# Moving the second scores and AV three matmuls later, giving group 0 a fourth output tile, and sharing the first half's products with GpSimd

## The chip, the cores and the metric

The kernel runs on one core of a Trainium2 chip. A core has five engines with instruction streams of their own: TensorE (PE in the profile, with its weight loads as PEld), VectorE (DVE), ScalarE (ACT), GpSimd (POOL) and SyncE (SP), which here only issues DMA transfers. The metric is the device time of one execution in microseconds (us). It was 322.27 us, the median of three runs (321.61 to 323.1).

## The reference: hourglass attention, then a feed-forward layer

The inputs are `q`, `k` and `v` of 8 batches, 8 heads, 576 positions and 64 elements a head. Two attentions are computed for each head and added:

```
q_d, k_d, v_d = means over 4 neighbouring positions     # 144 positions
out_up    = repeat(softmax(q_d @ k_d.T / 8) @ v_d, 4)   # back to 576
scores    = where(|i - j| < 4, q @ k.T / 8, -1e9)
out_local = softmax(scores) @ v                         # a band of 7
x = (out_up + out_local), heads side by side            # 4608 tokens x 512
out = (h * sigmoid(1.702 * h)) @ w_out, with h = x @ w_in   # 512 -> 2048 -> 512
```

The second part is the MoE of the names in the kernel, a feed-forward layer with one expert. Its matmuls are most of the work.

## The kernel before

**MoE.** The 4608 tokens are handled in nine groups of 512, 0 to 8. `mm1` multiplies `w_in` (the weights, 128 columns at a time: 16 blocks `ffc`) with `xT`, four matmuls of 128x128 by 512 a block, one for each of the four tensors `xT[0..3]` (`dmc`), which hold 128 columns of `x` each, transposed. ScalarE applies SiLU from PSUM into `gT` (L858). `mm2` multiplies `gT` with `w_out`: four output tiles of 128 tokens, 16 matmuls each (L919). `store` copies a tile from PSUM to a buffer `osb` on ScalarE (L904) and SP's queue writes it out (L909). There are three such buffers. One group is 128 of these matmuls.

**Attention.** Batch 0 is done at the start. Batch b is computed while group b - 1 runs its MoE, so groups 0 to 6 carry an attention and groups 7 and 8 do not. From group 1 on (batches 2 to 7) the steps are hung between MoE matmuls at the counts in `POS`: a count below 16 stands ahead of that block of `mm1`, a count of 16 + n ahead of matmul n of `mm2`. The five steps are: the scores of the first four heads (12), their Exp and mask (16), the scores, Exp and mask of the other four heads (33), the attention times V (AV) of the first half, `avx` for `xT[0]` and `xT[1]` (41), and of the second half, for `xT[2]` and `xT[3]` (53). Group 0 has counts of its own (`POS_0`) and another AV.

**PSUM.** Three pairs of banks, PA[0] to PA[2], serve the scores and AV. Each block of scores fills all three: the pooled scores in PA[0], the local ones in PA[1] and PA[2]. ScalarE empties them with one Exp for `ed` (L450) and two for `es` (L444), and VectorE multiplies `es` with the mask (L458). An AV block fills all three again, with numerators and denominators: PA[0] and PA[2] are the main parts (`mains(par)`), PA[1] is the rest. Two further banks, PM, and the PA banks take the MoE's sums.

**The tail of an AV block** (L758 to L791). ScalarE takes Ln of the denominators into `l` (L762, L764), and one Exp of -`l` over all 1440 columns makes their inverses (L768). VectorE copies the numerators into `n` (L763, L767); these copies are ordered behind the Ln that reads the same banks. `l` has two buffers, `n` one. Then nine products of `n` and `l` on VectorE (L773) make `od`, the pooled part, and the eight pieces of the two `xT`; two adds bring `od` into each `xT` (L789), on GpSimd for the first half and on VectorE for the second. After the second half ScalarE loads the table for SiLU again (L770). The next group's `mm1` reads `xT[0]` and `xT[1]` in its first eight matmuls, `xT[2]` in the next four, then `xT[3]`.

**Order.** Each engine works through its instructions in the order of the program; waits on other engines are added where data or buffers demand it. VectorE goes on with the transposes of the next batch's `k` and `q` (L284) behind the second half's adds; GpSimd sums them over four positions (L315, L319), issues the next loads, and prepares `vb` and `vd` (L325, L332, L335), which the next AV reads.

Of the kernel before, what the change touches and what calls it, by code (L numbers as in the profile page):

```python
# [8 lines left out]
FP32 = mybir.dt.float32  # L9
BF16 = mybir.dt.bfloat16  # L10
AF = mybir.ActivationFunctionType
ALU = mybir.AluOpType
# [7 lines left out]
def kernel(  # L20
# [9 lines left out]
    nc = tc.nc  # L30
    B, H, S, D = q.shape
# [655 lines left out]
    def avx(b, hps):  # L687
        vb, vd = vbs[b % 2], vds[b % 2]

        def mains(par):  # L690
            return PA[2 * par]

        def down(kc, den):
            for u, hp in enumerate(hps):
                rows = slice(64 * u, 64 * u + 48)
                for j in range(2):
                    nc.tensor.matmul(  # L697
                        mains(u)[64 * j : 64 * j + 64, den, DN : DN + SD],
                        lhsT=ones[rows, 1, :] if den else vd[rows, kc, hp // 2 * 2 + j, 0:D],
                        rhs=eds[hp // 2][rows, j, SD * kc : SD * kc + SD],  # L700
                        start=(kc == 0), stop=(kc == 2),
                        tile_position=(64 * u, 64 * j),
                    )

        def local(den, to, what):
            for par in range(2):
                hp = hps[par] if to == "main" else hps[1 - par]
                i, c0, ni, n = what[par]
                rows = slice(64 * par, 64 * par + 64)
                if to == "rest":  # L710
                    t, bk = PA[1], par
                    at = 256 * den + 57 * (i - 1 + par)
                else:
                    t, bk = mains(par), den
                    at = 57 * i + c0 if par == 0 else 57 * i
                    if to == "extra":
                        at = EX
                for j in range(2):
                    nc.tensor.matmul(  # L719
                        t[64 * j : 64 * j + 64, bk, at : at + ni * n],  # L720
                        lhsT=ones[rows, 0, :] if den else vb[rows, i, 2 * hp + j, 0:D],
                        rhs=sub(es[hp][rows, j, :], 60 * i + c0, (60, ni), (1, n)),
                        start=True, stop=True,
                        tile_position=(64 * par, 64 * j),
                    )

        def rest(k):
            local(0, "rest", ((k + 1, 3, 1, 57), (k, 0, 1, 57)))

        def rest_den(k):  # L730
            local(1, "rest", ((k + 1, 3, 2, 57), (k, 0, 2, 57)))

        def main(k):
            local(0, "main", ((k, 3 if k else 0, 1, 57 if k else 60),
                              (k, 0, 1, 57 if k < 4 else 60)))

        def extra(den):
            local(den, "extra", ((0, 0, 1, 60), (4, 0, 1, 60)))

        for kc in range(3):  # L740
            down(kc, 0)
            rest(kc)
            down(kc, 1)
            if kc < 2:
                rest_den(2 * kc)
        rest(3)
        main(0)
        local(1, "main", ((1, 3, 2, 57), (0, 0, 2, 57)))
        main(1)
        local(1, "main", ((3, 3, 2, 57), (2, 0, 2, 57)))  # L750
        main(2)
        local(1, "main", ((0, 0, 1, 60), (4, 0, 1, 60)))
        main(3)
        extra(0)
        main(4)
        extra(1)

        l = work.tile([128, 2, S + SD], FP32, name="l", tag="l", bufs=2)  # L758
        n = work.tile([128, 2, S + SD], FP32, name="n", tag="n", bufs=1)
        od = work.tile([128, 2, SD], FP32, name="od", tag="od", bufs=2)  # L760
        for par in range(2):
            nc.scalar.activation(out=l[:, par, 0:RS], in_=mains(par)[:, 1, 0:RS], func=AF.Ln)  # L762
            nc.vector.tensor_copy(out=n[:, par, 0:RS], in_=mains(par)[:, 0, 0:RS])  # L763
        nc.scalar.activation(  # L764
            out=l[:, :, RS : S + SD], in_=PA[1][:, :, 256 : 256 + S + SD - RS], func=AF.Ln
        )
        nc.vector.tensor_copy(out=n[:, :, RS : S + SD], in_=PA[1][:, :, 0 : S + SD - RS])  # L767
        nc.scalar.activation(out=l, in_=l, func=AF.Exp, scale=-1.0)  # L768
        if hps[0]:
            nc.scalar.preload_act_table_set("silu_and_others")  # L770

        def mult(out, *part):
            nc.vector.tensor_tensor(out=out, in0=sub(n, *part), in1=sub(l, *part), op=ALU.mult)  # L773

        t0, W = b * S, S + SD
        mult(od, DN, (W, 2), (1, SD))
        xa, xb = (xT[hp] for hp in hps)
        mult(sub(xa, t0 + 3, (114, 5), (1, 57)), 3, (57, 5), (1, 57))
        mult(sub(xa, t0 + 60, (114, 4), (1, 57)), W + RS, (57, 4), (1, 57))
        mult(sub(xa, t0 + 516, (1, 60)), W + EX, (1, 60))  # L780
        mult(sub(xa, t0, (1, 3)), 0, (1, 3))
        mult(sub(xb, t0 + 60, (114, 5), (1, 57)), W, (57, 5), (1, 57))
        mult(sub(xb, t0 + 117, (114, 4), (1, 57)), RS, (57, 4), (1, 57))
        mult(sub(xb, t0, (1, 60)), EX, (1, 60))
        mult(sub(xb, t0 + 573, (1, 3)), W + 285, (1, 3))
        for u, hp in enumerate(hps):
            xs = xT[hp][:, t0 : t0 + S].rearrange("p (t f) -> p t f", f=4)
            eng = nc.vector if hps[0] else nc.gpsimd
            eng.tensor_tensor(  # L789
                out=xs, in0=xs, in1=sub(od[:, u, :], 0, (1, SD), (0, 4)), op=ALU.add  # L790
            )  # L791

# [93 lines left out]
    def mm2(g, gT, steps):  # L886
        tok0 = g * TG
        turn["m"] = 1
        n = 0

        if g == 0:
            order = [(t0 + u, 4 * c + f)
                     for t0, c in ((0, 0), (0, 1), (2, 0), (2, 1),
                                   (0, 2), (2, 2), (0, 3), (2, 3))
                     for u in range(2) for f in range(4)]
        else:
            order = [(t, ffc) for t in range(4) for ffc in range(n_ffc)]
        ops = {}

        def store(t, ap, c0, n, eng, q):  # L900
            r0 = tok0 + 128 * t
            osb = moe_sb.tile([128, n], FP32, name="osb", tag=f"osb{n}", bufs=3)
            if eng is nc.scalar:
                eng.activation(out=osb, in_=ap, func=AF.Copy, scale=1.0 / GELU_SCALE)  # L904
            else:
                eng.tensor_single_scalar(  # L906
                    out=osb, in_=ap, scalar=1.0 / GELU_SCALE, op=ALU.mult
                )
            q.dma_start(out=out[r0 : r0 + 128, c0 : c0 + n], in_=osb)  # L909

        for t, ffc in order:
            if g == n_groups - 1 and t == 3:
                continue
            for f in steps.get(n, ()):
                f()
            n += 1
            if ffc == 0:
                ops[t] = PB[0][:, t - 2, :] if g == 0 and t > 1 else pm_tile()
            nc.tensor.matmul(  # L919
                ops[t],  # L920
                lhsT=gT[:, ffc, t * 128 : (t + 1) * 128],
                rhs=w_out_bf[:, ffc, :],
                start=(ffc == 0), stop=(ffc == n_ffc - 1),
            )
            if ffc == n_ffc - 1 and not (g == 0 and t == 2):
                for u in (2, 3) if g == 0 and t == 3 else (t,):
                    store(u, ops[u], 0, d_model, nc.scalar, nc.sync)

        if g == n_groups - 1:
            for h in range(2):  # L930
                cols = slice(256 * h, 256 * h + 256)
                p = pm_tile()
                for ffc in range(n_ffc):
                    nc.tensor.matmul(
                        p[:, 0:256],
                        lhsT=gT[:, ffc, 384:512],
                        rhs=w_out_bf[:, ffc, cols],
                        start=(ffc == 0), stop=(ffc == n_ffc - 1),
                    )
                if h == 0:  # L940
                    store(3, p[:, 0:256], 0, 256, nc.scalar, nc.sync)
                else:
                    store(3, p[:, 0:128], 256, 128, nc.scalar, nc.scalar)
                    store(3, p[:, 128:256], 384, 128, nc.vector, nc.sync)
        for f in steps.get(n, ()):
            f()

    POS = [12, 16, 33, 41, 53]
    POS_0 = [16, 18, 27, 46, 50, 55, 64, 68, 73]
    VDP_0 = 41  # L950

# [164 lines left out]
```

## Time and profile before

| what | us |
|---|---|
| median of three runs | 322.27 |
| the profiled execution | 321.51 |
| its span, first to last instruction | 319.7 |
| TensorE matmuls busy | 300.3 (94%) |
| ScalarE busy | 200.4 (63%) |
| GpSimd busy | 156.7 (49%) |
| VectorE busy | 143.0 (45%) |
| TensorE's granted clock, mean | 0.993 |

The engines work side by side, so their busy times do not add up. Lines of the profile name the source line, the engine, the operation, and output <- input by the program's names; "x8" counts instructions in a line, and a bracket tells how long the engine had been idle and what ended that. In a timeline the first two numbers are the start, in us from the span's start, and the time to the last end of the merged instructions. In the list of waits they are the total, the count and the longest. In the list of instruction groups the numbers behind the bar are the busy time in us, the mean of one in ns, and the idle time ahead.

### The profile page before, as it was taken

The numbers are of one execution on the slowest core, as the hardware profiler recorded it, in microseconds if no ns is written. First come the engines' busy times: TensorE is split into PE (matmuls) and PEld (weight loads), VectorE is DVE, ScalarE is ACT, GpSimd is POOL, SyncE is SP. The second block draws the span as 40 slices with busy tenths as digits, with TensorE's granted clock in tenths as the row PEclk, the third lists the DMA queues.
The fourth block names the chain that finished last, engine by engine and source line by source line (L and its number), as shares of the span: only waits on it lengthen the run. The fifth ranks groups of instructions, "written<-read, shape, count | busy, mean of one in ns | idle before, by whom it ended". The sixth has DMA issues, their size and how long they took to land.

```text
span 319.7 us, 10088 instructions
## 1 busy us (share of the span) xinstructions
PE 300.3 (94%) x4389; PEld 153.9 (48%) x4434; DVE 143.0 (45%) x283; ACT 200.4 (63%) x321; POOL 156.7 (49%) x183
## 2 busy tenths in 40 slices
PE   6779998989999999999999999999999999999995
PEld 2454454434554555454545454545454544444444
DVE  6973524740299048903791379226931580000000
ACT  4474782366795589558856875687577758315611
POOL 8973960099334973398239913992298030000000
PEclk9989999999999999999999999999999999999999
DMA  6999999979705991399349934794330120020011
GB/s 118 122 203 211 173 131 213 202 198 225 150 35 165 195 190 49 126 205 172 98 129 191 196 83 125 167 198 107 107 110 3 53 84 2 9 89 35 0 66 66
DMA packets 64124, 39.98 MB, mean 125 GB/s; under 512 B 44624, under 2 KB 54992, under 8 KB 64080
## 3 DMA queue, kind: packets, MB, share of 16 engines
q0 software_dynamic: 18864, 14.95, 33.1%
q1 hardware_dynamic: 45072, 24.32, 30.6%
q8 instruction: 34, 0.56, 0.7%
q14 instruction: 10, 0.08, 0.1%
q10 hardware_dynamic: 144, 0.07, 0.1%
HBM read 44.83 MB, written 9.44 MB: 170 GB/s over the span
## 4 chain that ended last, share of the span: by engine, by line
PE 75%; DMA 9%; ACT 6%; POOL 5%; issue 4%; DVE 0%; POOLq 0%; ACTq 0%
PE pm L919 28%; PE pm L847 22%; PE pa L847 12%; DMA kb<-in_k_dram 4%; PE pa L409 3%; PE pa L719 2%; DMA qb<-in_q_dram 2%; ACT es L444 2%; ACT L813 2%; PE pa L697 2%; PE pa L919 2%; ACT ed L450 2%; POOL vb L237 2%; DMA vb<-in_v_dram 1%; PE pa L433 1%
## 5 line engine op out<-in xcount | busy, mean ns | idle before, releaser
L919 PE MATMUL pm<-w_out_bf,gT 128*128 128x512 bf16 x503 | 114.6, 379 | 3.3 <-issue 2.9
L847 PE MATMUL pm<-xT,w_in_bf 128*128 128x512 bf16 x361 | 92.2, 380 | 1.7 <-ACT gT L858 1.3
L847 PEld LDWEIGHTS <-w_in_bf 128*128 128x128 bf16 x576 | 55.6, 98 | 67.7 <-issue 1.7
L858 ACT ACTIVATE gT<-pm 128x512 bf16<-128x512 f32 x94 | 56.2, 602 | 42.9 <-PE pm L847 42.9
L919 PEld LDWEIGHTS <-gT 128*128 128x128 bf16 x560 | 52.6, 98 | 60.9 <-issue 0.2
L458 DVE TENSOR_TENSOR es<-es,mask 128x600 bf16<-128x600 bf16 x28 | 19.8, 722 | 89.7 <-ACT es L444 89.0
L847 PE MATMUL pa<-xT,w_in_bf 128*128 128x512 bf16 x199 | 53.2, 379 | 0.4
L904 ACT ACTIVATE osb<-pm 128x512 f32<-128x512 f32 (+2 forms) x35 | 20.4, 582 | 33.1 <-PE pm L919 27.6
L789 POOL TENSOR_TENSOR xT<-xT,od 128x576 bf16<-128x576 bf16 x12 | 16.8, 1396 | 43.9 <-DVE xT L773 43.6
L315 POOL TENSOR_TENSOR pq<-kT 128x576 f32<-128x576 bf16 x14 | 16.2, 1157 | 39.0 <-DVE kT L284 38.9
L858 ACT ACTIVATE gT<-pa 128x512 bf16<-128x512 f32 x50 | 29.0, 607 | 5.6 <-PE pa L847 5.6
L773 DVE TENSOR_TENSOR xT<-n,l 128x285 bf16<-128x285 f32 (+1 forms) x96 | 28.2, 366 | 0.0
L906 DVE TENSOR_SCALAR osb<-pm 128x128 f32<-128x128 f32 x1 | 0.3, 292 | 53.7 <-ACT osb L904 53.7
L332 POOL TENSOR_TENSOR pq<-v 112x512 f32<-112x512 f32 x18 | 23.7, 1318 | 0.0
L444 ACT ACTIVATE es<-pa 128x600 bf16<-128x600 f32 x32 | 19.7, 670 | 2.1 <-PE pa L391 2.1
L284 DVE STREAM_TRANSPOSE kT<-kb 128x576 f32<-128x576 f32 x16 | 19.9, 1247 | 1.6 <-DMA kb<-in_k_dram 1.5
L284 DVE STREAM_TRANSPOSE qT<-qb 128x576 f32<-128x576 f32 x16 | 19.9, 1241 | 0.3 <-DMA qb<-in_q_dram 0.2
L763 DVE COPY n<-pa 128x492 f32<-128x492 f32 x24 | 15.0, 665 | 8.9 <-ACT l L762 8.3
L762 ACT ACTIVATE l<-pa 128x492 f32<-128x492 f32 x24 | 12.6, 578 | 10.0 <-PE pa L719 10.0
L450 ACT ACTIVATE ed<-pa 128x864 bf16<-128x864 f32 x16 | 14.3, 891 | 4.5 <-PE pa L433 4.4
L768 ACT ACTIVATE l<-l 128x1440 f32<-128x1440 f32 x12 | 16.8, 1403 | 0.4
L237 POOL DMA_DIRECT2D vb<-in_v_dram x20 | 13.8, 701 | 5.3 <-DMA w_in_bf<-in_moe_w_in_dram 3.3
(119 smaller groups left out, 353.6 us busy)
## 6 DMA issues: line engine op xcount, KB each, us to landing
out_dram<-osb SPq DMA_DIRECT2D x35, 256.0 KB, 2.4
vf<-in_v_dram SPq DMA_DIRECT2D x60, 128.0 KB, 6.3
v<-in_v_dram SPq DMA_DIRECT2D x72, 96.0 KB, 3.2
kb<-in_k_dram POOLq DMA_DIRECT2D x16, 288.0 KB, 6.5
qb<-in_q_dram POOLq DMA_DIRECT2D x16, 288.0 KB, 8.5
w_out_bf<-in_moe_w_out_dram POOLq DMA_DIRECT2D x4, 512.0 KB, 13.7
vb<-in_v_dram POOLq DMA_DIRECT2D x20, 64.0 KB, 5.4
w_in_bf<-in_moe_w_in_dram POOLq DMA_DIRECT2D x2, 512.0 KB, 8.1
```

Source lines behind the costliest of these rows:

```text
L237: nc.gpsimd.dma_start(out=vbs[b % 2][64 * par : 64 * par + 64, i, :, 0:D], in_=bass.AP(tensor=v.tensor, offset=v[b, 0].offset + (114 * i + ...
L284: nc.vector.transpose(out=t32.rearrange("p (i c) -> p c i", c=18), in_=store[b, qd].bitcast(FP32).rearrange("p (c d) -> p c d", c=18),)
L332: eng.tensor_tensor(out=t1[0:112], in0=x[:, :, 0:2, :], in1=x[:, :, 2:4, :], op=ALU.add)
L444: nc.scalar.activation(out=es[2 * qd + u][:, :, 0:300], in_=sp[u][:, :, 0:300], func=AF.Exp, scale=inv_sqrt_d,)
L450: nc.scalar.activation(out=eds[qd][:, :, 0:432], in_=sd[:, :, 0:432], func=AF.Exp, scale=inv_sqrt_d / 16.0,)
L458: nc.vector.tensor_tensor(out=ev, in0=ev, in1=mask, op=ALU.mult)
L768: nc.scalar.activation(out=l, in_=l, func=AF.Exp, scale=-1.0)
L773: nc.vector.tensor_tensor(out=out, in0=sub(n, *part), in1=sub(l, *part), op=ALU.mult)
L847: nc.tensor.matmul(acc, lhsT=w_in_bf[:, dmc, ffc * 128 : (ffc + 1) * 128], rhs=xT[dmc][:, g * TG : g * TG + TG], start=(dmc == 0), stop=(d ...
L858: nc.scalar.activation(out=gT[:, ffc, :], in_=acc, func=AF.Silu, scale=GELU_SCALE)
L904: eng.activation(out=osb, in_=ap, func=AF.Copy, scale=1.0 / GELU_SCALE)
L919: nc.tensor.matmul(ops[t], lhsT=gT[:, ffc, t * 128 : (t + 1) * 128], rhs=w_out_bf[:, ffc, :], start=(ffc == 0), stop=(ffc == n_ffc - 1),)
```

## The change

Three counts of `POS` grow by three, so the second scores and both AV blocks of groups 1 to 6 come three MoE matmuls later. In group 0 the third output tile is copied into the buffer of `n`, which group 0 does not otherwise use, so that four output tiles have four buffers. In the AV tail, the first half (`second` false) alternates Ln and copies over the bank pairs and gives `od`, the four pieces of `xT[1]` and the two adds to GpSimd; VectorE keeps the four pieces of `xT[0]`. The second half (`second` true) keeps all products and adds on VectorE, and its Exp of -`l` is done in two parts. TensorE's instructions stay the same in number; GpSimd gets 30 more, VectorE 30 fewer, ScalarE six more.

```diff
-        for par in range(2):
+        second = hps[0] > 0
+        W = S + SD
+
+        def ln_main(par):
             nc.scalar.activation(out=l[:, par, 0:RS], in_=mains(par)[:, 1, 0:RS], func=AF.Ln)
+
+        def ln_rest():
+            nc.scalar.activation(
+                out=l[:, :, RS:W], in_=PA[1][:, :, 256 : 256 + W - RS], func=AF.Ln
+            )
+
+        def copy_main(par):
             nc.vector.tensor_copy(out=n[:, par, 0:RS], in_=mains(par)[:, 0, 0:RS])
-        nc.scalar.activation(
-            out=l[:, :, RS : S + SD], in_=PA[1][:, :, 256 : 256 + S + SD - RS], func=AF.Ln
-        )
-        nc.vector.tensor_copy(out=n[:, :, RS : S + SD], in_=PA[1][:, :, 0 : S + SD - RS])
-        nc.scalar.activation(out=l, in_=l, func=AF.Exp, scale=-1.0)
-        if hps[0]:
+
+        def copy_rest():
+            nc.vector.tensor_copy(out=n[:, :, RS:W], in_=PA[1][:, :, 0 : W - RS])
+
+        def inverse(c0, c1):
+            ap = l[:, :, c0:c1]
+            nc.scalar.activation(out=ap, in_=ap, func=AF.Exp, scale=-1.0)
+
+        if second:
+            ln_main(0)
+            ln_main(1)
+            inverse(0, RS)
+            ln_rest()
+            inverse(RS, W)
             nc.scalar.preload_act_table_set("silu_and_others")
-
-        def mult(out, *part):
-            nc.vector.tensor_tensor(out=out, in0=sub(n, *part), in1=sub(l, *part), op=ALU.mult)
-
-        t0, W = b * S, S + SD
-        mult(od, DN, (W, 2), (1, SD))
+            copy_main(0)
+            copy_main(1)
+            copy_rest()
+        else:
+            ln_main(0)
+            copy_main(1)
+            ln_main(1)
+            copy_rest()
+            ln_rest()
+            copy_main(0)
+            inverse(0, W)
+
+        def mult(eng, out, *part):
+            eng.tensor_tensor(out=out, in0=sub(n, *part), in1=sub(l, *part), op=ALU.mult)
+
+        t0 = b * S
         xa, xb = (xT[hp] for hp in hps)
-        mult(sub(xa, t0 + 3, (114, 5), (1, 57)), 3, (57, 5), (1, 57))
-        mult(sub(xa, t0 + 60, (114, 4), (1, 57)), W + RS, (57, 4), (1, 57))
...
+        ea = nc.vector
+        eb = nc.vector if second else nc.gpsimd
+        mult(eb, od, DN, (W, 2), (1, SD))
+        mult(ea, sub(xa, t0 + 3, (114, 5), (1, 57)), 3, (57, 5), (1, 57))
+        mult(ea, sub(xa, t0 + 516, (1, 60)), W + EX, (1, 60))
+        mult(ea, sub(xa, t0, (1, 3)), 0, (1, 3))
+        if second:
+            mult(ea, sub(xa, t0 + 60, (114, 4), (1, 57)), W + RS, (57, 4), (1, 57))
+        mult(eb, sub(xb, t0 + 60, (114, 5), (1, 57)), W, (57, 5), (1, 57))
+        mult(eb, sub(xb, t0, (1, 60)), EX, (1, 60))
+        mult(eb, sub(xb, t0 + 573, (1, 3)), W + 285, (1, 3))
+        if not second:
+            mult(ea, sub(xa, t0 + 60, (114, 4), (1, 57)), W + RS, (57, 4), (1, 57))
+        mult(eb, sub(xb, t0 + 117, (114, 4), (1, 57)), RS, (57, 4), (1, 57))
         for u, hp in enumerate(hps):
             xs = xT[hp][:, t0 : t0 + S].rearrange("p (t f) -> p t f", f=4)
-            eng = nc.vector if hps[0] else nc.gpsimd
-            eng.tensor_tensor(
+            eb.tensor_tensor(
                 out=xs, in0=xs, in1=sub(od[:, u, :], 0, (1, SD), (0, 4)), op=ALU.add
             )
...
         def store(t, ap, c0, n, eng, q):
             r0 = tok0 + 128 * t
-            osb = moe_sb.tile([128, n], FP32, name="osb", tag=f"osb{n}", bufs=3)
+            if g == 0 and t == 2:
+                osb = work.tile([128, 2, S + SD], FP32, name="n", tag="n", bufs=1)
+                osb = osb[:, 0, 0:n]
+            else:
+                osb = moe_sb.tile([128, n], FP32, name="osb", tag=f"osb{n}", bufs=3)
...
-    POS = [12, 16, 33, 41, 53]
+    POS = [12, 16, 36, 44, 56]
```

More of the change, by code (lines that the diff above doesn't have):

```diff
@@ L780, in avx @@
[L780 to L785, printed above, removed]
+        def ln_rest():
+            nc.scalar.activation(
+                out=l[:, :, RS:W], in_=PA[1][:, :, 256 : 256 + W - RS], func=AF.Ln
+            )
```

## The prediction

> **What bounds the kernel now.** I read the page first, then who waited for whom on TensorE, the chain that ended last, and the timelines of one group (group 3, whose MoE starts at 129.6 us) engine by engine.
>
> ```profile
> span 319.7 us, 10088 instructions
> PE 300.3 (94%) x4389; PEld 153.9 (48%) x4434; DVE 143.0 (45%) x283; ACT 200.4 (63%) x321; POOL 156.7 (49%) x183
> ...
> PE pm L847 <- ACT gT L858: 1.3, 1, 1.3
> PE pa L409 <- ACT es L444: 0.9, 6, 0.2
> ```
>
> TensorE is busy for 94% of the span, so the change can win only what TensorE still waits for. The first wait line is one wait of 1.3 us, the second comes once in each of six groups. The chain shows what the first stands behind:
>
> ```profile
> 61.23 3.37 DMA out_dram<-osb
> 64.68 0.60 ACT osb L904
> 65.81 7.71 PE pm L847 x35
> ```
>
> Group 0 has four output tiles and three buffers. The fourth copy waits for a buffer until the first tile has been written out, holds up ScalarE, and with it the first SiLU of group 1. Now the second wait, in the PE and ACT timelines:
>
> ```profile
> 147.19 1.24 PE L919 MATMUL pm<-w_out_bf,gT 128*128 128x512 bf16 x5
> 148.77 0.22 PE L409 MATMUL pa<-qT,kT 32*64 32x60 bf16 x4 [0.15 <-ACT es L444]
> 150.08 1.67 PE L919 MATMUL pm<-w_out_bf,gT 128*128 128x512 bf16 x7 [0.16 <-issue]
> ...
> 147.50 1.23 ACT L444 ACTIVATE es<-pa 128x600 bf16<-128x600 f32 x2
> ```
>
> The second scores reach TensorE at 148.27 but need the banks that the two Exp leave at 148.73. Counted between MoE matmul starts, less the slots of 0.216 us, the first scores cost 1.13 us of TensorE (groups 1 to 6 agree), the second 1.56, 1.62, 1.59, 1.57, 1.59, 1.48. So the wait is worth 0.44 us a group, 2.62 us in all. The two AV blocks cost 1.21 and 1.20 us: no wait is left in them.
>
> The third thing to see is the tail, from the first AV block to the next group's xT:
>
> ```profile
> 156.30 2.85 DVE L773 TENSOR_TENSOR xT<-n,l 128x285 bf16<-128x285 f32 x8
> 159.25 1.25 DVE L763 COPY n<-pa 128x492 f32<-128x492 f32 x2
> 161.32 1.83 DVE L773 TENSOR_TENSOR xT<-n,l 128x285 bf16<-128x285 f32 x8
> 163.07 1.42 DVE L789 TENSOR_TENSOR xT<-xT,od 128x576 bf16<-128x576 bf16 x2
> ...
> 157.34 1.35 POOL L789 TENSOR_TENSOR xT<-xT,od 128x576 bf16<-128x576 bf16 x1 [6.06 <-DVE xT L773]
> 159.23 1.21 POOL L789 TENSOR_TENSOR xT<-xT,od 128x576 bf16<-128x576 bf16 x1 [0.54 <-DVE xT L773]
> ...
> 164.15 0.38 PE L847 MATMUL pm<-xT,w_in_bf 128*128 128x512 bf16 x1
> ```
>
> The same eight products take 1.83 us alone and 2.85 us while GpSimd adds: one 228-element product that begins at 157.54 lasts 1.40 us instead of 0.39, until GpSimd's add is over. VectorE and GpSimd, with two SBUF operands each, run one after the other. The second half's xT2 is ready at 163.82, and the next group's matmul that reads it starts at 164.15. The tail has 0.33 us to spare and no more.
>
> **The change, part by part.** Times are from A, the start of the MoE matmul behind the first AV block (152.79 in group 3).
>
> Output tile. ScalarE is free at 63.95 instead of 65.28. The first SiLU then waits only for its matmuls (their end, 64.33), runs 0.60 us, and TensorE goes on at 65.01 instead of 65.81. The rest of that stop (64.38 to 65.01) stays, since group 1 begins with two banks. Gain 0.80 us; bounds 0 and 1.4 (the whole stop). SP's queue keeps its order. `n` is a single buffer, so group 1's first copy waits for that store, which has 20 us to land: nothing.
>
> Second scores. They come 3 slots (0.65 us) later, at 148.92, behind the Exp's end at 148.73. The wait goes: gain 2.62 us, bounds 0 and 2.62. What is late next: the first AV block, still eight matmuls behind, wants bank PA2, which the second scores' Exps leave. They start 0.82 us after the scores (149.83), take 2.02 us (149.63 to 151.65 before), and end at 151.85; AV starts at 151.87. I take 0.02 us a group, bounds 0 and 0.3.
>
> AV later. Both blocks move with the scores, 12 matmuls apart as before, but only 24 instead of 27 matmuls follow the second. So xT2 is needed at A + 12 x 0.2163 + 1.20 + 24 x 0.2163 + 8 x 0.2163 = A + 10.72, against A + 11.36 before.
>
> Reading the banks. In the first half Ln and copies now take turns on a bank pair. VectorE starts with ScalarE instead of behind it: last copy at A + 2.0 instead of A + 2.5, and the second AV starts at A + 2.69. Ln waits for copies in turn, so the Exp ends at A + 3.37 instead of A + 3.04. Products start 0.09 later, as before: A + 3.45.
>
> Products. VectorE keeps 4 (half of the 8 at 161.32, 0.88 us), GpSimd gets five, 288, 285, 60, 3 and 228 elements. The trace has no such product on GpSimd. The nearest rows:
>
> ```profile
> L319 POOL TENSOR_TENSOR qdT<-pq 128x288 bf16<-128x288 f32 x13 | 8.7, 667 | 1.0
> L332 POOL TENSOR_TENSOR pq<-v 112x512 f32<-112x512 f32 x18 | 23.7, 1318 | 0.0
> L335 POOL TENSOR_TENSOR vd<-pq 112x256 bf16<-112x256 f32 x18 | 13.5, 753 | 1.4
> ```
>
> From L319 (667 ns for 288) and the undisturbed L789 (1.21 us for 576), 1.9 ns an element and 0.12 us fixed, the five sum to 2.25 us, and 2.09 with the 0.04 us by which independent GpSimd operations overlap. From L335 and L332 (undisturbed 0.73 and 1.27: 2.1 ns an element and 0.19 fixed) it is 2.62. I take 2.3, nearer L319, which has 128 partitions and 288 elements. Then the blocking by VectorE's four: from 0 to all their 0.88 us. The first L789 loses 0.14 or 0.60 us (1.35 or 1.81 instead of 1.21) when it meets one or three products; I take 0.5. So the five end 2.8 us after they begin, bounds 2.1 and 3.5: A + 6.25.
>
> Who waits for that: `n` is single, so VectorE's first copy of the second half waits for GpSimd's last product, and behind it stand all copies, products and adds of that half. It starts at A + 6.33 (0.08 for the signal). Before, it started at 159.25, A + 6.46, so sharing brings almost nothing. From there to xT2 it took 4.57 us (159.25 to 163.82). New: GpSimd's adds run from A + 6.25 to A + 8.63, and VectorE's first product of the second half wants to start at A + 8.03. The 228-element case above started in effect 0.14 before GpSimd's add ended, so this one starts at A + 8.49, 0.46 late. xT2: 6.33 + 4.57 + 0.46 = A + 11.36, TensorE at A + 11.41 with 0.05 for the signal, against 10.72. A new stop of 0.69 us a group, bounds 0 (products in 2.1) and 1.4 (in 3.5). xT3 follows 0.67 later, and the four matmuls on xT2 take 0.87: no more. xT0 and xT1 (A + 8.63) are needed at A + 8.98 and 9.2: hidden.
>
> Exp in parts, second half. Two Exp cost one more start, some 0.15 us on ScalarE, and `l` is ready long before VectorE gets to it. The last-but-one output copy ends about A + 8.95 against the next group's start at A + 8.98. That cover is thin, but the stop on xT2 stands behind it and swallows 0.1 us. GpSimd's next-batch work starts 0.28 us later behind the transposes; `vd` then ends some 0.3 us before the first AV instead of 0.4. Neither costs anything.
>
> Sum: -0.80 - 2.62 + 6 x 0.02 + 6 x 0.69 = +0.84 us.
>
> The Trainium skill's GPSIMD Engine Reference, § Elementwise — side-by-side cycle accounting, has about 2.6 cycles an element for two inputs; on 864 elements at its 1.2 GHz that is an estimate of 1.87 us, and with 0.5 of blocking the stop would be 0.25 us a group and the sum -1.8 us. L332's 2.1 ns an element agrees, but the starts come on top. The skill's SBUF — State Buffer, § Who interferes with whom, speaks against sharing at all: a VectorE instruction with two SBUF inputs and a GpSimd one that reads SBUF exclude each other, and the second to issue waits for the whole of the first. The 1.40 us product agrees; the add of 1.81 us, which let two later products by, does not keep to issue order.
>
> **The sum against the runs.** The profiled execution took 321.51 us (span 319.7 and 1.8 around it), 0.76 below the median of 322.27. The sum is a difference; I put it on the median: 323.1 us.
>
> **Rivals.** (1) Faster: the five products finish in 2.1 us, because small GpSimd operations are cheap and VectorE's four fall into the gaps between them. The tail then keeps up, and -0.80 - 2.62 + 0.12 leaves 319.0 us. For it: L319's short 667 ns. Against: every meeting of the two engines in the trace costs GpSimd 0.1 to 0.6 us. It decides below 2.3 us for the five. (2) Clearly slower: the slow price (2.62) and VectorE's products all let through first (0.88), 3.5 us; the stop is 1.4 us a group, sum +5.1, 327.4 us. For it: three of six first adds lost 0.60 us. Against: the other three lost 0.14. It decides from 2.9 us on. (3) The moved scores find a new wait: PA2 comes 0.3 us late for the first AV block, in all groups; with the rest as forecast, 324.8 us. For it: a margin of 0.02 us. Against: the Exps' times hardly vary.
>
> **How the numbers follow.** A measurement of this kernel tells about 0.5%, 1.6 us, from no change: 320.7 to 323.9. The forecast (stops of 0.4 to 1.0 us, 321.3 to 325.0) gets 0.42: 0.27 within, 0.12 slower, 0.03 faster. Rival 1 gets 0.20, nearly all faster; rival 2 0.28, nearly all slower; rival 3 0.10, 0.07 slower and 0.03 within. Together: faster 0.22, same 0.32, slower 0.46. The range runs from rival 1's time to just short of rival 2's: 319.0 to 327.0.
>
> **What would show it.** In the profile after: no TensorE wait of the second scores for `es` and 1.13 us for them; group 1 resuming near 65.0; GpSimd's five products over some 2.8 us; VectorE's first `n` copy of the second half starting with GpSimd's last product; that half's `od` product over 0.8 us long; and, in groups 2 to 7, TensorE stopped ahead of its ninth matmul by `xT` from VectorE. If that last wait is missing, the pricing of the products is wrong; if TensorE stops ahead of AV, rival 3 holds.

## The result, and the profile after

The changed kernel takes 324.36 us (median, 323.49 to 325.89), the kernel before beside it 322.6 us. The ratio is 1.006 with a 95% interval of 1.0031 to 1.009: slower by 1.0 to 2.9 us, where the forecast had 0.8 us and 323.1 us. The profiled execution was the longest of the nine, 325.89 us, with a span of 323.9 us.

The two profiled executions differ by 4.4 us, and the change is not all of it. The rest lies ahead of group 1, and the windows of TensorE show that the two were not alike there. Columns: stretch in us, its length, PE busy (instructions), granted clock, DMA share, GB/s. First the kernel before:

```profile
23.00:30.00 7.00, 6.78 (x62) 0.86 1.11 211
30.00:62.00 32.00, 29.37 (x585) 1.00 1.33 173
62.00:190.00 128.00, 123.77 (x2008) 1.00 0.69 153
```

The same stretches of the kernel after:

```profile
23.00:30.00 7.00, 7.00 (x95) 0.62 1.12 212
30.00:62.00 32.00, 31.11 (x572) 1.00 1.32 175
62.00:190.00 128.00, 125.30 (x1967) 1.00 0.71 153
```

Group 0's first MoE matmul starts at 24.59 us instead of 23.44, between 23 and 30 us the clock granted in this execution was 0.62 instead of 0.86, and group 1 begins at 63.85 us instead of 62.65. Attention of batch 0 and group 0 up to there hold almost none of the change (the fourth output tile is copied at their end). From 30 us on both have the full clock. So I compare the stretch from group 1's first MoE matmul to the last MoE matmul: 253.19 us before, 256.15 after, **+2.96 us**. Stops inside it are counted as in the prediction: between the starts of neighbouring MoE matmuls, less the slots of 0.216 us.

The list of waits of TensorE (total, count, longest) has lost `es` and gained one:

```profile
PE pm L880 <- DVE xT L822: 4.5, 6, 0.8
...
PE pm L880 <- ACT gT L891: 0.5, 1, 0.5
```

The second line is what is left of the stop between groups 0 and 1. Counted between starts it was 1.44 us before and is 0.63 now. The first line is the new stop that was forecast, once in each of groups 2 to 7. Here it is in the timeline of TensorE (start, time to the last end, what it is, and idle time ahead), behind group 3:

```profile
164.99 0.59 PE L880 MATMUL pa<-xT,w_in_bf 128*128 128x512 bf16 x2
166.33 0.38 PE L880 MATMUL pm<-xT,w_in_bf 128*128 128x512 bf16 x1 [0.74 <-DVE xT L822]
```

Two slots after 164.99 would be 165.42; the ninth matmul starts at 166.33, 0.91 us late. The six stops are 0.91, 0.91, 0.90, 0.92, 0.90 and 0.91 us, 5.45 in all. (The bracket and the wait list say less, since the ends of matmuls are modelled.)

VectorE in the same tail; A, the start of the MoE matmul behind the first AV block, is 154.64 here:

```profile
158.06 2.18 DVE L802 TENSOR_TENSOR xT<-n,l 128x285 bf16<-128x285 f32 x4 [1.48 <-ACT l L780]
161.23 1.25 DVE L773 COPY n<-pa 128x492 f32<-128x492 f32 x2 [0.99 <-POOL xT L802]
162.40 0.62 DVE L776 COPY n<-pa 128x456 f32<-128x456 f32 x1
162.94 0.92 DVE L802 TENSOR_TENSOR od<-n,l 128x288 f32<-128x288 f32 x1
163.78 1.83 DVE L802 TENSOR_TENSOR xT<-n,l 128x285 bf16<-128x285 f32 x8
165.53 1.41 DVE L822 TENSOR_TENSOR xT<-xT,od 128x576 bf16<-128x576 bf16 x2
```

And GpSimd:

```profile
158.10 1.06 POOL L802 TENSOR_TENSOR od<-n,l 128x288 f32<-128x288 f32 x1 [4.88 <-ACT l L780]
159.13 2.07 POOL L802 TENSOR_TENSOR xT<-n,l 128x285 bf16<-128x285 f32 x4
161.16 2.37 POOL L822 TENSOR_TENSOR xT<-xT,od 128x576 bf16<-128x576 bf16 x2
```

VectorE's four products need 2.18 us instead of the 0.88 that the prediction gave them undisturbed, GpSimd's five 3.10 us. VectorE idles 0.99 us until GpSimd's last one is done at 161.20, because both read the single `n`. Then the second half runs to xT2 at 166.27, A + 11.63, while TensorE wanted it at A + 10.72.

The stretch adds up from its parts:

| part | forecast, us | measured, us |
|---|---|---|
| stop between groups 0 and 1 | -0.80 | -0.81 |
| second scores, groups 1 to 6 (9.42 before, 7.29 after) | -2.62 | -2.13 |
| AV blocks | +0.12 | about 0 |
| stop ahead of the ninth matmul, six times | +4.14 | +5.45 |
| 0.05 us ahead of each of six groups' first matmul | in the line above | +0.32 |
| sum | +0.84 | +2.8 (the stretch itself: +2.96) |

### The profile page after: what moved, and what is told of

Same layout as the page of the kernel before. It is cut to its first block, busy times and chain, and to the rows that moved or that the text cites. A ratio compares the mean times of both kernels' runs of the same rounds, so it can differ in the third digit from the quotient of the medians.

```text
span 323.9 us, 10130 instructions
## 1 busy us (share of the span) xinstructions
PE 307.8 (95%) x4434; PEld 154.0 (48%) x4434; DVE 135.4 (42%) x253; ACT 202.6 (63%) x327; POOL 173.0 (53%) x213
## 4 chain that ended last, share of the span: by engine, by line
PE 72%; DVE 9%; POOL 6%; ACT 5%; DMA 4%; issue 3%; POOLq 0%
PE pm L880 24%; PE pm L956 21%; PE pa L880 12%; POOL xT L802 4%; DVE n L773 4%; DVE xT L802 3%; ACT l L780 3%; PE pa L409 3%; PE pa L956 2%; DMA qb<-in_q_dram 2%; POOL od L802 2%; PE pa L433 2%; DMA vb<-in_v_dram 2%; DVE xT L822 1%; PE pa L719 1%
## 5 line engine op out<-in xcount | busy, mean ns | idle before, releaser
L956 PE MATMUL pm<-w_out_bf,gT 128*128 128x512 bf16 x528 | 119.6, 379 | 0.0
L880 PE MATMUL pm<-xT,w_in_bf 128*128 128x512 bf16 x376 | 94.9, 382 | 4.9 <-DVE xT L822 4.5
L458 DVE TENSOR_TENSOR es<-es,mask 128x600 bf16<-128x600 bf16 x28 | 15.9, 571 | 94.8 <-ACT es L444 93.9
L802 DVE TENSOR_TENSOR xT<-n,l 128x285 bf16<-128x285 f32 (+1 forms) x72 | 24.1, 400 | 8.9 <-ACT l L780 8.9
L802 POOL TENSOR_TENSOR od<-n,l 128x288 f32<-128x288 f32 x6 | 6.4, 1066 | 34.8 <-ACT l L780 34.8
L332 POOL TENSOR_TENSOR pq<-v 112x512 f32<-112x512 f32 x18 | 23.7, 1316 | 0.0
L765 ACT ACTIVATE l<-pa 128x492 f32<-128x492 f32 x24 | 13.3, 580 | 8.8 <-PE pa L719 7.9
L780 ACT ACTIVATE l<-l 128x1440 f32<-128x1440 f32 (+2 forms) x18 | 18.1, 1004 | 0.6
```

Of the source, the lines that this page charges most:

```text
L332: eng.tensor_tensor(out=t1[0:112], in0=x[:, :, 0:2, :], in1=x[:, :, 2:4, :], op=ALU.add)
L458: nc.vector.tensor_tensor(out=ev, in0=ev, in1=mask, op=ALU.mult)
L780: nc.scalar.activation(out=ap, in_=ap, func=AF.Exp, scale=-1.0)
L802: eng.tensor_tensor(out=out, in0=sub(n, *part), in1=sub(l, *part), op=ALU.mult)
L880: nc.tensor.matmul(acc, lhsT=w_in_bf[:, dmc, ffc * 128 : (ffc + 1) * 128], rhs=xT[dmc][:, g * TG : g * TG + TG], start=(dmc == 0), stop=(d ...
L956: nc.tensor.matmul(ops[t], lhsT=gT[:, ffc, t * 128 : (t + 1) * 128], rhs=w_out_bf[:, ffc, :], start=(ffc == 0), stop=(ffc == n_ffc - 1),)
```

## The experiments

**The theory** after this: the moved scores and AV take 0.65 us from the tail's time; sharing the first half's products makes the tail longer, through GpSimd's price, the turns that the two engines take, and the buffer `n`, for which the second half waits. The main rivals: the later AV alone causes the stops (A), and the turns alone lengthen the tail, so that the wait for `n` only stands where another would stand (C; the texts put on record call it the shared port). Each run below is given by its median, its ratio to the kernel before, and the stretch from group 1 on in its profile.

### The output tile alone

```diff
+            if g == 0 and t == 2:
+                osb = work.tile([128, 2, S + SD], FP32, name="n", tag="n", bufs=1)
+                osb = osb[:, 0, 0:n]
+            else:
-            osb = moe_sb.tile([128, n], FP32, name="osb", tag=f"osb{n}", bufs=3)
+                osb = moe_sb.tile([128, n], FP32, name="osb", tag=f"osb{n}", bufs=3)
```

> The kernel before with nothing but the fourth output tile in the buffer of n. Theory (tail: the first half's products on GpSimd take 3.1 us beside VectorE's, hold the single n, and so bring xT2 0.9 us late): this part is a gain by itself, TensorE's stop at the start of group 1 shrinks from 1.44 to 0.63 us, -0.8 us in all, no stop before the ninth matmul of groups 2 to 7. Rival A (the AV blocks three matmuls later make the tail late, whoever multiplies): the same -0.8 us. Rival B (the store into n delays the first tail of group 1): a wait of VectorE's first n copy for a DMA in group 1 and less than 0.5 us won.

Measured: 319.82 us, 0.9944 (0.9924 to 0.9964), stretch 252.39 us, -0.80. Group 1's start in the timeline of TensorE:

```profile
61.23 1.89 PE L847 MATMUL pm<-xT,w_in_bf 128*128 128x512 bf16 x8
63.59 2.10 PE L847 MATMUL pm<-xT,w_in_bf 128*128 128x512 bf16 x9 [0.47 <-ACT gT L858]
```

Eight slots after 61.23 would be 62.96; TensorE goes on at 63.59, a stop of 0.63 us as forecast (64.38 to 65.01 there). So against this profile of the kernel before the first part is worth its 0.80 us; the next run shows that the stop it shortens is not the same in every execution. Of the later groups only group 7 now stops ahead of its ninth matmul, for 0.10 us. The ratio speaks of 1.2 to 2.4 us. Group 1 begins 1.42 us earlier than in the profile of before, and the clock of the stretch from 23 to 30 us was 1.00 here against 0.86. The copy that was changed comes behind that stretch. The later runs show the same: in every kernel with the new output tile the ratio speaks of 1.0 to 1.8 us less than the stretch, in the one without it of 1.2 us more. So about 1 us of the medians lies outside the stretch, and what the output tile, or where it lies, has to do with it is open.

### The moved scores and AV alone

```diff
-    POS = [12, 16, 33, 41, 53]
+    POS = [12, 16, 36, 44, 56]
```

> The kernel before with nothing but the three counts of POS raised by three. Theory: xT2 is ready at A + 11.0 as before but is needed at A + 10.7, a stop of 0.3 to 0.4 us before the ninth matmul of groups 2 to 7 (2.1 us), against some 2.1 to 2.6 us won at the second scores: -0.5 to +0.3 us, even with before. Rival A: the stop is the 0.9 us of the changed kernel, and the whole is +3 us.

Measured: 322.42 us, 1.0031 (1.0006 to 1.0055), stretch 253.03 us, -0.16. The old tail against the nearer deadline, on TensorE:

```profile
163.28 0.59 PE L847 MATMUL pa<-xT,w_in_bf 128*128 128x512 bf16 x2
164.08 0.38 PE L847 MATMUL pm<-xT,w_in_bf 128*128 128x512 bf16 x1 [0.20 <-DVE xT L789]
```

Two slots after 163.28 would be 163.71, so the stop is 0.37 us; the six are 0.34 to 0.39, 2.2 us together. They give back a little more than the 1.9 us that the second scores win. That the stretch is still 0.16 us shorter comes from a part that this run didn't touch, the stop between groups 0 and 1:

```profile
62.95 1.89 PE L847 MATMUL pm<-xT,w_in_bf 128*128 128x512 bf16 x8
65.52 2.75 PE L847 MATMUL pm<-xT,w_in_bf 128*128 128x512 bf16 x12 [0.68 <-ACT gT L858]
```

Eight slots after 62.95 would be 64.68, so this stop is 0.84 us, where the profile of the kernel before has 1.44 with the same three buffers: ScalarE waited 0.63 us for the first tile's write instead of 1.24. Against this execution the new output tile would win only 0.21 us. How the stop varies over more executions isn't known.

The deadline moved by 0.65 us and the old tail had 0.33 to spare: 0.32 was to be expected. Rival A is right that the move makes a stop, but for 0.37 of the 0.91 us only; the rest needs the sharing.

### The sharing, without the move

```diff
-    POS = [12, 16, 36, 44, 56]
+    POS = [12, 16, 33, 41, 53]
```

> The changed kernel with the counts of POS as before (33, 41, 53). Theory: xT2 still comes at A + 11.65 and is now needed at A + 11.36, so a stop of 0.3 us stays before the ninth matmul of groups 2 to 7 (1.8 us) and the second scores' wait is back; with the tile's -0.8 it is +0.5 to +1.5 us against before. Rival A: no stop, -0.8 us against before.

Measured (the diff is against the changed kernel): 322.07 us, 1.0004 (0.9977 to 1.0031), stretch 254.40 us, +1.21. The list of waits has both the new stop and the old wait:

```profile
PE pm L880 <- DVE xT L822: 1.0, 6, 0.2
```

```profile
PE pa L409 <- ACT es L444: 0.9, 6, 0.2
```

With the old deadline the shared tail is still 0.31 to 0.33 us late in each group. So it is about 0.6 us longer than the old one, which had 0.33 to spare. A tail 0.6 us longer and a deadline 0.65 us nearer, less the 0.33 to spare, make the 0.91 us.

### The products not shared

```diff
-        eb = nc.vector if second else nc.gpsimd
+        eb = nc.vector
...
-            eb.tensor_tensor(
+            (nc.vector if second else nc.gpsimd).tensor_tensor(
```

> The changed kernel with all nine products of the first half back on VectorE (the two adds stay on GpSimd). Theory: VectorE is through with them at about A + 5.6 (start A + 3.45, 2.1 us, the adds start only behind the eighth), the second half's first n copy follows at once instead of at A + 6.6, and TensorE stops 0 to 0.3 us before the ninth matmul instead of 0.91: -3.3 to -5.5 us against the changed kernel, some 2 us faster than before. Rival A: the stop stays at 0.7 to 0.9 us and the time is that of the changed kernel within 1 us.

Measured: 318.01 us (316.94 to 318.89), 0.989 (0.9868 to 0.9912), stretch 250.80 us, -2.39. VectorE's timeline (A = 150.56; the trace lacks the record of that matmul, as it does in the kernel before, and the next one starts a slot later, at 150.78):

```profile
154.03 0.46 DVE L802 TENSOR_TENSOR od<-n,l 128x288 f32<-128x288 f32 x1 [1.53 <-ACT l L780]
154.40 1.83 DVE L802 TENSOR_TENSOR xT<-n,l 128x285 bf16<-128x285 f32 x8
156.34 1.25 DVE L773 COPY n<-pa 128x492 f32<-128x492 f32 x2
...
158.04 0.75 DVE L802 TENSOR_TENSOR od<-n,l 128x288 f32<-128x288 f32 x1
```

On GpSimd are only the adds:

```profile
156.01 2.46 POOL L822 TENSOR_TENSOR xT<-xT,od 128x576 bf16<-128x576 bf16 x2 [7.09 <-DVE xT L802]
```

VectorE does nine products alone, 0.46 and 1.83 us, in less time than the 3.10 us in which the two engines did them together. The second half begins at A + 5.78 instead of A + 6.59, xT2 is ready at A + 10.65, 0.07 us ahead of its need, and the stop ahead of the ninth matmul is gone from all groups. Everything else of the change is still there, so the sharing alone costs 5.35 us of the stretch (256.15 less 250.80), and without it the change makes the kernel faster. This tail is also faster than that of the kernel before, where the eight pieces took 2.85 us: three products of `xT[1]` stand ahead of the last of `xT[0]` here, so GpSimd's first add, into `xT[0]`, begins only at 156.01, when VectorE's products are nearly done.

### GpSimd's products undisturbed

```diff
+            if eng is nc.scalar:
+                eng.copy(out=out, in_=sub(n, *part))
+                return
...
-        ea = nc.vector
+        ea = nc.vector if second else nc.scalar
```

> The changed kernel with VectorE's four products of the first half replaced by plain copies on ScalarE, so that the factor l is left out for these pieces of xT0; VectorE then reads nothing from SBUF while GpSimd multiplies. It measures GpSimd's own price. Theory: five products in 2.1 to 2.6 us instead of 3.1, the rest is waiting for VectorE's four; the stop before the ninth matmul falls by the same 0.5 to 0.9 us. Rival D (no blocking, GpSimd is simply slow on these shapes): the five still take 3.0 us or more and the stop stays at 0.9 us.

This one, a single execution of 323.2 us, has ScalarE copy the four pieces of `xT[0]`, and leaves the factor `l` out of them. GpSimd's timeline:

```profile
156.44 0.79 POOL L805 TENSOR_TENSOR od<-n,l 128x288 f32<-128x288 f32 x1 [5.21 <-ACT l L780]
157.20 1.84 POOL L805 TENSOR_TENSOR xT<-n,l 128x285 bf16<-128x285 f32 x4
159.00 2.38 POOL L825 TENSOR_TENSOR xT<-xT,od 128x576 bf16<-128x576 bf16 x2
```

The five products take 2.60 us alone (156.44 to 159.04): 0.79, 0.78, 0.31, 0.19 and 0.66 us for 288, 285, 60, 3 and 228 elements. Beside VectorE's four it was 3.10, so the blocking is 0.50 us. Its time isn't a clean number for the tail, since a new wait appears (list of TensorE's waits):

```profile
PE pm L883 <- ACT osb L944: 3.4, 6, 0.6
```

ScalarE's extra work delays the last output copies and with them each group's first matmul, by 0.73 to 0.74 us. The tail's own lateness, with xT2 at A + 11.13, is hidden behind that.

### A second `n`

```diff
+    n2 = persist.tile([128, 2, S + S // 4], FP32, name="n2")
...
-        n = work.tile([128, 2, S + SD], FP32, name="n", tag="n", bufs=1)
+        n = n2 if hps[0] else work.tile([128, 2, S + SD], FP32, name="n", tag="n", bufs=1)
```

(To make room, three constants of the setup become views of `n2`, and the smaller output buffers get fewer copies.)

> The changed kernel with a second buffer for n in the second half (room made by laying start-up constants into it and by fewer buffers for the last group's small output tiles). Theory: VectorE no longer waits for GpSimd's last product; its copies start at about A + 4.5 instead of A + 6.6 and the stop of 0.91 us before the ninth matmul goes or shrinks to at most 0.4, held there only by products that run into GpSimd's; 3 to 5.5 us faster than the changed kernel. Rival C (the shared port alone sets the tail): copies start early but the products wait behind GpSimd's adds until A + 9, and the stop stays at 0.6 us or more.

Measured: 323.84 us, 1.0036 (1.0006 to 1.0066), stretch 255.47 us, +2.28; the stops are still 0.76 to 0.82 us. VectorE (A = 153.50):

```profile
156.98 2.18 DVE L804 TENSOR_TENSOR xT<-n,l 128x285 bf16<-128x285 f32 x4 [1.48 <-ACT l L782]
159.08 1.24 DVE L775 COPY n<-pa 128x492 f32<-128x492 f32 x2
...
160.78 0.82 DVE L804 TENSOR_TENSOR od<-n,l 128x288 f32<-128x288 f32 x1
161.53 2.84 DVE L804 TENSOR_TENSOR xT<-n,l 128x285 bf16<-128x285 f32 x8
164.28 1.42 DVE L824 TENSOR_TENSOR xT<-xT,od 128x576 bf16<-128x576 bf16 x2
```

GpSimd beside it:

```profile
158.05 2.06 POOL L804 TENSOR_TENSOR xT<-n,l 128x285 bf16<-128x285 f32 x4
160.08 2.59 POOL L824 TENSOR_TENSOR xT<-xT,od 128x576 bf16<-128x576 bf16 x2
```

The wait for `n` is gone: the copies start at A + 5.58, 1.01 us earlier. But the products behind them now meet GpSimd's adds in full: `od` still takes 0.82 us (0.92 in the changed kernel, 0.45 undisturbed), and the eight pieces 2.84 instead of 1.83. Of the 1.01 us, 0.92 is lost again, and xT2 comes at A + 11.54 instead of A + 11.63. My theory expected the stops to shrink with this wait; that was wrong, and C was right. The buffer orders the work, but behind it the wait for GpSimd's turns is nearly as long.

### The moves and the tile, with another order of products

The old tail on VectorE, with the pieces of `xT[1]` ahead of those of `xT[0]` in the first half, so that the first add (into `xT[0]`) is released by the last product:

```diff
+        def a_parts():
...
+        def b_parts():
...
+        for f in (a_parts, b_parts) if hps[0] else (b_parts, a_parts):
+            f()
...
-    POS = [12, 16, 33, 41, 53]
+    POS = [12, 16, 36, 44, 56]
```

`a_parts` holds the four products for `xT[0]` (or `xT[2]`), `b_parts` those for the other; the fourth output tile is as in the change.

> The kernel before with the fourth tile, the counts raised by three, and the first half's pieces of xT1 multiplied ahead of those of xT0, all on VectorE, so that GpSimd's first add starts behind VectorE's products instead of among them. Theory: VectorE is through with the products at A + 5.3 instead of A + 6.4, the second half's xT2 is ready at A + 10.4, needed at A + 10.7: no stop before the ninth matmul, and the gains of tile (0.8) and scores (2.1) stay: -2.5 to -3.3 us against before. Rival A: a stop of 0.5 us or more and no gain over before.

Measured: 317.6 us (316.44 to 319.33), 0.9866 (0.9825 to 0.9908), stretch 250.63 us, -2.56. VectorE (A = 151.58):

```profile
154.71 0.46 DVE L773 TENSOR_TENSOR od<-n,l 128x288 f32<-128x288 f32 x1 [0.62 <-ACT l L768]
155.09 1.83 DVE L773 TENSOR_TENSOR xT<-n,l 128x285 bf16<-128x285 f32 x8
157.02 1.25 DVE L763 COPY n<-pa 128x492 f32<-128x492 f32 x2
...
158.73 0.96 DVE L773 TENSOR_TENSOR od<-n,l 128x288 f32<-128x288 f32 x1
```

GpSimd's adds:

```profile
157.00 2.37 POOL L795 TENSOR_TENSOR xT<-xT,od 128x576 bf16<-128x576 bf16 x2 [7.03 <-DVE xT L773]
```

TensorE at the next group's ninth matmul, without a stop:

```profile
161.86 0.59 PE L853 MATMUL pa<-xT,w_in_bf 128*128 128x512 bf16 x2
162.29 0.38 PE L853 MATMUL pm<-xT,w_in_bf 128*128 128x512 bf16 x1
```

The eight products take 1.83 us instead of the 2.85 of the kernel before, because GpSimd's adds begin only behind them and then meet copies from PSUM. xT2 is ready at A + 10.53, ahead of A + 10.72. With 1.3% below the kernel before it has the lowest median of the kernels run, though not clear of the 318.01 us of the kernel that doesn't share; both give GpSimd none of the products.

## Why the prediction came out as it did

The side and the mechanism were right: a stop of TensorE ahead of its ninth matmul, by xT2 from VectorE, in groups 2 to 7. The median lies 1.3 us above the forecast, inside the range. That it lies so near is in part luck: in the stretch, which holds all the terms of the sum, +0.84 us became +2.96, and the medians differ by less only because about 1 us was gained outside it, which no term foresaw and no run explains. Step by step:

**Output tile.** Forecast -0.80 us, measured -0.81 in the change and -0.80 alone, all against one profile of the kernel before. With the 0.84 us stop of the run with the counts alone it would have been -0.21, so the size of this term rests on how long the first tile's write took in that execution.

**Second scores.** The wait for `es` is gone, as forecast, but -2.62 came out as -2.13 us. The prediction put all six to 1.13 us; they cost 1.26, 1.21, 1.13, 1.27, 1.28 and 1.13. What takes the 0.1 us in four of the six was not settled. They reach TensorE about 0.19 us behind the end of the Exps in all six groups, so it isn't the old wait. Group 1's first scores, which the change leaves where they were, vary as much: 1.13 us before, 1.23 with the output tile alone and 1.25 with the counts alone.

**First AV.** +0.02 us a group was allowed for; the blocks cost 1.20 and 1.19 to 1.20 us as before. The third rival, a late PA2, did not happen, though its margin was 0.02 us.

**Products on GpSimd.** This is the term that was mis-sized. I took 2.3 us for the five, nearer the row of L319; beside ScalarE's copies, with VectorE idle, they take 2.60 us, which is the 2.62 that L332 and L335 gave. I chose L319 for its 128 partitions and 288 elements; that was the wrong neighbour. The added blocking was taken as 0.5 and measured 0.50. So the five end 3.10 us after they begin, where 2.8 was forecast, and the second half's first copy starts at A + 6.59 instead of A + 6.33. That 0.26 is nearly all of the difference between A + 11.63 and A + 11.36 for xT2, and it is why the groups lose 0.96 us each (0.91 ahead of the ninth matmul, 0.05 ahead of the first) instead of 0.69: 5.77 us for 4.14.

The Trainium skill's GPSIMD Engine Reference, § Elementwise — side-by-side cycle accounting, gave an estimate of 1.87 us for the 864 elements. The runs have 2.60 us. From 228 to 288 elements the time grows by about 2.1 ns an element, and the rate that the Trainium skill gives is an estimate of 2.2, but 60 elements take 0.31 us and 3 take 0.19. With five instructions the starts are a good part of the difference; a rate an element is not enough for short ones.

**The second half behind it.** 4.57 us from copy to xT2 plus 0.46 for the blocked `od`: measured 166.27 less 161.23, 5.04 us, with `od` at 0.92 instead of 0.45. Right.

**The single `n`.** The prediction made the wait for `n` the carrier of the delay. As an account of the order it held. As a cause it did not: with a second `n` only 0.09 us was won. What remains is the time for which the two engines keep each other off. Their work in the first half, 0.88 us of VectorE and 2.60 of GpSimd, lasted 3.10 us together, not 2.60. It was not the full sum of 3.48 either: VectorE's first product took its undisturbed 0.46 us although GpSimd's first began 0.04 us behind it.

The Trainium skill's SBUF — State Buffer, § Who interferes with whom, says that a VectorE instruction with two SBUF inputs and a GpSimd one that reads SBUF exclude each other. The traces agree for the most part: 2.18 for 0.88 us of VectorE beside GpSimd's products, 2.84 for 1.83 with the second `n` beside the adds, and 1.83 where GpSimd is idle. The copies from PSUM take 1.25 us with GpSimd's adds beside them and 1.24 to 1.25 elsewhere. This sentence of the Trainium skill was the best argument against the change; the forecast took its price of the blocking from the trace and saw that sharing brings almost nothing, but not that it costs 5.35 us against VectorE alone with the adds out of its way.

**Exp in parts.** The cover was called thin, and it was: 0.05 us ahead of each group's first matmul, for ScalarE's output copies, is there in this kernel, in the one with a second `n` and in the one that doesn't share, and neither in the two that move the counts and keep the old tail on ScalarE, nor in the one that has the new tail and the old counts. Here the stop on xT2 stands behind it and swallows it, as forecast, since it is xT2's time that ends both. In the kernel that doesn't share, no such stop is left and the 0.05 us counts. So it takes the new tail and the move together. The Exp in parts and the alternation of Ln and copies were not tried apart, so which of them makes it is open.

**The rivals.** Five products in 2.1 us was out by 0.5 even before any blocking. The slow case, 3.5 us, took the right price for the products and too much blocking.

## What to carry to other kernels

Moving work later on the bounding engine pays only if what hangs behind it has the time: here the move alone won about 2 us at the second scores, and taking 0.65 us a group from a tail with 0.33 to spare cost 2.2. Before elementwise work with two SBUF operands is shared between VectorE and GpSimd, look in the trace for a product that grew while the other engine was busy: if they exclude each other, the slower engine's price comes on top, and a second buffer only moves the wait. An order in which GpSimd's part is released when VectorE turns to copies from PSUM is worth more; here that order in place of the sharing, with the same move and tile, gave -1.3% where the change gave +0.6%.

## What was not expected of the hardware

A product of 3 elements a partition takes 0.19 us on GpSimd and one of 60 takes 0.31, against 0.79 for 288. Splitting work for GpSimd into odd pieces is dear.

Freeing one resource bought 0.09 of 1.01 us, because the next in the row was held just as long.

The granted clock at the start varied between the profiled executions, 0.62 to 1.00 in the 7 us from 23 us on, and the start of group 1 between 61.23 and 63.85 us. The latest start came with the lowest clock, but the clock is not the whole of it: the four executions with 1.00 (the output tile alone, not shared, undisturbed, another order) start group 1 at 61.23, 61.49, 62.57 and 62.42 us. That spread is as much as the change itself, so time differences of single executions had to be taken from group 1 on.
